# Linear attention plus gated feed-forward on one core: features kept token-major, turns moved from TensorE to DMA, key-value sums accumulated over all tiles, residual added by VectorE, start rebuilt

## Chip, cores and metric

One core of a Trainium2 chip. The time is the device time of one execution in microseconds (us), lower is better.

## The reference

One input x (2048 tokens of 512, bf16) is layer-normalised and goes into two branches whose results are added to x.

```python
xn = layernorm(x)
# branch A: 32 heads of 16
q, k, v = split_heads(xn @ wqkv)                       # wqkv 512 x 1536
pq, pk = q @ w_phi[h], k @ w_phi[h]                    # w_phi 16 x 16 per head
phi_q = concat(softmax(pq), softmax(-pq))              # 32 features per head
phi_k = concat(softmax(pk), softmax(-pk))
kv = phi_k.T @ v ;  z = sum over tokens of phi_k       # per head: 32 x 16 and 32
o = (phi_q @ kv) / (phi_q @ z + 1e-6)
A = o @ wo                                             # 512 x 512
# branch B
B = ((xn @ w_gate) * (xn @ w_up)) @ w_down             # 512 -> 1792 -> 512
out = x + A + B
```

## The kernel before

It is already tuned: a helper records each operation with its reads and writes, and a list scheduler orders the engines. Tokens are handled in 16 tiles of 128. `w_phi` is folded into `wqkv` on the chip, so one matmul group gives pq or pk. The parts that matter here:

Words used below: a *turn* is a transpose; a *unit* is the gate product, the up product and their elementwise product for one of the 14 feature tiles and 512 (or 256) tokens; the *numerator* of a tile is its `phi_q @ kv`; *K steps* are the key tiles' stretch of the program, and the *hand-over* is the point where it passes to the query tiles (the q stage). A *hole* is a time in which TensorE waits, and *filler* is work that may be put there. In the profiles PE is TensorE, PEld its weight loads, DVE VectorE, ACT ScalarE, POOL GpSimd and SP the queue that issues DMA.

```python
# (1) normalisation: statistics of four tiles, then a Newton iteration on GpSimd (cut)
for it in range(3):
    pool(... tv = src * src); pool(... tv = tv * veps)
    pool(... tv = tv * -0.5 + 1.5); pool(... yv = src * tv)

# (2) x, the projection weights, the q features and o are all turned on TensorE
def emit_xT(t):
    for q in range(NQ):
        items.append((bank(b, q * 128, 128), xn_tile(t)[:, q * 128:(q + 1) * 128], ident))
    mm_multi(items)
    act_op(out_ap, bank(b)...)                         # eviction on ScalarE

# (3) key-value sums: all 16 key tiles first, then 8 groups of 16 matmuls, 129 wide
for t in range(NT):
    pairs.append((ek_v[:, side, t, c * 128:(c + 1) * 128], vext_all[:, t, c, :]))
mm_group(out_ap, pairs)                                # out_ap: 128 x 129

# (4) per query tile: 8 turns, 8 numerators (128 wide), 8 denominators (8 wide), 4 turns of o
for side in range(2):
    src = ering(slot, 0) if side == 0 else enr(slot)
    ... items.append((bank(tb[side], c * 128, 128), src[:, c * 128:(c + 1) * 128], ident))
for c in range(NQ):
    mm_group(bank(bo, c * 128, 128), [(eT_all[:, r, side * 4 + c, :], kvbd_v[:, c * 2 + side, :]) for side in range(2)])
for c in range(NQ):
    mm_group(bank(tb[0], c * 8, 8), [(eT_all[:, r, side * 4 + c, :], zbd_v[:, c * 2 + side, :]) for side in range(2)])

# (5) output: 14 down products, 4 of wo, and the residual as identity x x, in one accumulator
n_terms = NF + NQ + 1
for i, t in enumerate(tiles):
    acc_mm(i, ident, x_tile(t))
```

Of the 14 feature tiles of the gated branch five are computed early in units of 512 tokens; the other nine come in units of 256 tokens just before their down products.

The softmax here doesn't subtract the row's maximum and nothing guards it: scores larger than these inputs give would overflow.

## Time and profile before

| | before |
|---|---|
| time, median of the first 3 runs | 270.84 us (269.82 to 273.06) |
| span of the profiled execution | 270.5 us |
| TensorE busy | 246.2 us, 91% |
| VectorE, ScalarE, GpSimd busy | 58%, 47%, 20% |

From the page of the kernel before: the busy table; TensorE (PE), its granted clock and DMA in 40 slices (each digit is tenths); and the shares of the chain of work that ended last.

```profile
span 270.5 us, 4879 instructions
PE 246.2 (91%) x1902; PEld 156.7 (58%) x1936; DVE 156.2 (58%) x364; ACT 128.1 (47%) x261; POOL 53.8 (20%) x99
PE   0068999999999999999999999999999999999994
PEclk9999999999999999999999999999999999999999
DMA  6999300000000000000000001001001010000101
...
PE 80%; DVE 8%; ACT 3%; DMA 3%; issue 3%; POOL 2%; DVEq 0%; POOLq 0%
```

PE is the limit from the fifth slice on, at full clock. The table of stretches of the same kernel shows what is lost before that (columns: stretch, its length, busy us and instructions of each engine, granted clock, DMA share, GB/s):

```profile
0.00:14.90 14.90, 0.01 (x1) 0.01 (x1) 10.14 (x36) 1.28 (x1) 8.00 (x38) 1.00 0.88 282
14.90:38.00 23.10, 19.71 (x148) 12.91 (x151) 11.11 (x33) 18.84 (x36) 7.84 (x31) 1.00 0.66 240
...
180.00:268.00 88.00, 86.21 (x571) 55.39 (x579) 24.37 (x54) 21.59 (x53) 0.00 (x0) 1.00 0.05 16
```

In the first 38 us the trace has 112 transposes (at 56 ns, 6.3 us of streaming) and 36 matmuls of 512 columns (at 216 ns, 7.8 us): about 14 us of work at full rate, an estimate from the counts and the spacing below. A 128-wide record lasts 240 ns on average where neighbours can start 56 ns apart, so small matmuls that alternate with evictions look busy. The clock column reads 1.00 where the trace has no clock record yet, and the first one is at 27.24 us. The starts of neighbouring transposes lie 107 ns apart until 26.7 us and 56 ns apart from 27.9 us on: half rate, then full. Eight transposes before and after (start, length):

```profile
14.89 1.04 PE L323 MATMUL ps<-arena 128*128 128x128 bf16 x8 [14.89 <-POOL arena L450]
101.77 0.61 PE L323 MATMUL ps<-arena 128*128 128x128 bf16 x8
```

The spacing of matmuls is read where the chain runs through PE without a break. From the chain of the kernel before, in order of time (start, length, what):

```profile
186.99 2.68 PE ps L654 x12
189.67 0.87 PE ps L309 x8
```

L654 are 512 columns wide (223 ns each here; the median distance of neighbouring starts in the trace is 216), L309 here 256 (109 ns each).

### The profile page before, as it was taken

How to read it: one execution, taken by the hardware profiler on the slowest of the kernel's cores; microseconds unless marked ns; L12 is line 12 of the kernel's file. 1: busy time of each engine (PE TensorE's matmuls, PEld its weight loads, DVE VectorE, ACT ScalarE, POOL GpSimd, SP SyncE). 2: the span in 40 equal slices, each digit the busy share in tenths (PEclk: the TensorE clock that was granted, in tenths of full speed). 3: DMA queues.
4: the chain of work that ended last, by engine and by line, in shares of the span. 5: the costliest groups of instructions: out<-in, count | busy, mean ns of one | idle time of the engine just before them, and what ended most of it. 6: DMA issues, size and time to landing. Idle time of an engine off the chain costs nothing.

```text
span 270.5 us, 4879 instructions
## 1 busy us (share of the span) xinstructions
PE 246.2 (91%) x1902; PEld 156.7 (58%) x1936; DVE 156.2 (58%) x364; ACT 128.1 (47%) x261; POOL 53.8 (20%) x99
## 2 busy tenths in 40 slices
PE   0068999999999999999999999999999999999994
PEld 0046544444444587777567765775766757566661
DVE  3951699989797985787677776542232323313231
ACT  1057898646665704776665755632222313222221
POOL 4560253333442430313112131100000000000000
PEclk9999999999999999999999999999999999999999
DMA  6999300000000000000000001001001010000101
GB/s 198 351 393 381 119 0 1 2 0 0 0 0 2 0 4 2 0 2 0 22 19 2 4 1 41 0 2 39 0 2 39 2 39 0 26 15 2 39 1 39
DMA packets 9446, 12.12 MB, mean 45 GB/s; under 512 B 448, under 2 KB 8400, under 8 KB 9424
## 3 DMA queue, kind: packets, MB, share of 16 engines
q1 hardware_dynamic: 9392, 11.80, 12.6%
q8 instruction: 15, 0.25, 0.4%
q0 software_dynamic: 32, 0.02, 0.1%
q14 instruction: 7, 0.06, 0.1%
HBM read 9.72 MB, written 2.10 MB: 44 GB/s over the span
## 4 chain that ended last, share of the span: by engine, by line
PE 80%; DVE 8%; ACT 3%; DMA 3%; issue 3%; POOL 2%; DVEq 0%; POOLq 0%
PE ps L309 50%; PE ps L654 24%; PE ps L323 7%; ACT arena L287 3%; DMA arena<-in_A_w_phi_dram 3%; DVE arena L499 2%; DVE arena L506 1%; DVE arena L534 1%; DVE arena L504 1%; POOL arena L395 1%; DVE arena L465 1%; DVE arena L576 0%; DVE arena L679 0%; DVE arena L457 0%; POOL arena L449 0%
## 5 line engine op out<-in xcount | busy, mean ns | idle before, releaser
L287 ACT ACTIVATE arena<-ps 128x512 bf16<-128x512 f32 (+1 forms) x260 | 126.9, 541 | 138.9 <-PE ps L309 92.9
L309 PE MATMUL ps<-arena 128*128 128x256 bf16 (+4 forms) x1300 | 172.6, 279 | 1.6 <-ACT arena L287 0.5
L309 PEld LDWEIGHTS ps<-arena 128*128 128x128 bf16 x1312 | 109.0, 98 | 59.0 <-PE ps L309 2.2
L654 PE MATMUL ps<-arena 128*128 128x512 bf16 x282 | 77.9, 381 | 2.0 <-DVE arena L679 0.6
L679 DVE TENSOR_TENSOR arena<-ps,arena 128x256 bf16<-128x256 f32 x72 | 30.0, 416 | 55.3 <-PE ps L654 52.9
L323 PE MATMUL ps<-arena 128*128 128x128 bf16 x320 | 30.9, 240 | 17.6 <-POOL arena L450 14.9
L654 PEld LDWEIGHTS ps<-arena 128*128 128x128 bf16 x304 | 28.0, 97 | 24.4 <-PE ps L654 4.4
L323 PEld LDWEIGHTS ps<-arena 128*128 128x128 bf16 x320 | 24.4, 107 | 27.1 <-DMA arena<-in_A_wqkv_dram 14.9
L506 POOL TENSOR_TENSOR arena<-arena 128x512 bf16<-128x512 bf16 x16 | 22.6, 1413 | 34.6 <-DVE arena L504 26.3
L584 POOL TENSOR_TENSOR arena<-arena 128x512 bf16<-128x512 bf16 x16 | 16.9, 1056 | 63.0 <-DVE arena L582 47.0
L576 DVE TENSOR_REDUCE arena<-arena 128x32 f32<-128x512 bf16 x32 | 20.6, 678 | 7.3 <-ACT arena L287 7.2
L499 DVE TENSOR_REDUCE arena<-arena 128x32 f32<-128x512 bf16 x32 | 20.6, 678 | 6.0 <-ACT arena L287 6.0
L534 DVE TENSOR_TENSOR arena<-ps,arena 128x512 bf16<-128x512 f32 x20 | 13.6, 682 | 1.5 <-PE ps L309 1.4
L432 DVE BATCH_NORM_STATS2 arena<-arena 128x6 f32<-128x512 bf16 x16 | 10.5, 684 | 4.8 <-DMA arena<-in_A_x_dram 4.8
L707 DVE CAST arena<-ps 128x512 bf16<-128x512 f32 x8 | 5.5, 692 | 12.4 <-PE ps L654 12.3
L506 DVE TENSOR_TENSOR arena<-arena 128x512 bf16<-128x512 bf16 x16 | 11.6, 728 | 0.4
L465 DVE TENSOR_SCALAR arena<-arena 128x512 bf16<-128x512 bf16 x16 | 5.8, 410 | 9.8 <-PE ps L323 9.8
L621 DVE TENSOR_TENSOR arena<-ps,arena 128x512 bf16<-128x512 f32 x16 | 10.9, 682 | 0.3
L504 DVE RECIPROCAL arena<-arena 128x64 f32<-128x64 f32 x16 | 8.8, 550 | 0.4
L618 DVE SCALAR_TENSOR_TENSOR arena<-arena,ps 128x32 f32<-128x32 f32 x16 | 3.0, 188 | 10.3 <-PE ps L309 10.1
L620 DVE RECIPROCAL arena<-arena 128x32 f32<-128x32 f32 x16 | 5.6, 351 | 0.4
L581 DVE RECIPROCAL arena<-arena 128x32 f32<-128x32 f32 x16 | 5.6, 348 | 0.4
(31 smaller groups left out, 30.3 us busy)
## 6 DMA issues: line engine op xcount, KB each, us to landing
arena<-in_A_x_dram SPq DMA_DIRECT2D x4, 512.0 KB, 6.6
out_dram<-arena SPq DMA_DIRECT2D x16, 128.0 KB, 1.7
arena<-in_B_w_gate_dram SPq DMA_DIRECT2D x1, 1792.0 KB, 12.0
arena<-in_B_w_up_dram SPq DMA_DIRECT2D x1, 1792.0 KB, 15.2
arena<-in_B_w_down_dram SPq DMA_DIRECT2D x1, 1792.0 KB, 18.1
arena<-in_A_wqkv_dram SPq DMA_DIRECT2D x3, 512.0 KB, 11.2
arena<-in_A_wo_dram SPq DMA_DIRECT2D x1, 512.0 KB, 8.9
arena<-in_A_w_phi_dram POOLq DMA_DIRECT2D x1, 16.0 KB, 7.5
```

What stands on the lines that cost most here:

```text
L287: return e.activation(out=out_ap, in_=in_ap, func=func, scale=scale, **kw)
L309: ins = e.matmul(out_ap, lhsT=l, rhs=r, start=(i == 0), stop=(i == n - 1))
L323: ins = e.matmul(o, lhsT=l, rhs=r, start=True, stop=True)
L499: dve(lambda e, side=side: e.tensor_reduce(out=sm[:, side * 32:(side + 1) * 32], in_=ering(slot, side).rearrange("p (h f) -> p h f", f=16) ...
L504: dve(lambda e: e.reciprocal(out=rs, in_=sm), [sm], [rs])
L506: fn = (lambda e, side=side: e.tensor_tensor(out=ek_v[:, side, t, :].rearrange("p (h f) -> p h f", f=16), in0=ering(slot, side).rearrange( ...
L534: dve(lambda e: e.tensor_tensor(out=dest_ap, in0=bank(bu), in1=gring(slot), op=ALU.mult), [bank(bu), gring(slot)], [dest_ap])
L576: dve(lambda e, side=side: e.tensor_reduce(out=sm[:, side * 32:(side + 1) * 32], in_=ering(slot, side).rearrange("p (h f) -> p h f", f=16) ...
L584: pool(lambda e: e.tensor_tensor(out=enr(slot).rearrange("p (h f) -> p h f", f=16), in0=ering(slot, 1).rearrange("p (h f) -> p h f", f=16) ...
L621: dve(lambda e: e.tensor_tensor(out=oring(slot).rearrange("p (h d) -> p h d", d=16), in0=bank(bo).rearrange("p (h d) -> p h d", d=16), in1 ...
L654: return e.matmul(o, lhsT=lhsT, rhs=rhs, start=first, stop=last)
L679: dve(lambda e: e.tensor_tensor(out=h, in0=bank(bu, 256, 256), in1=g, op=ALU.mult), [bank(bu, 256, 256), g], [h])
```

## The change

The intent: take everything off TensorE that is not a product of the reference. Features of both signs are made side by side in one 1024-wide token-major tile, reduced once, and turned by one DMA per tile; x (from tile 4 on), o and the projection weights are turned by DMA too. Key-value sums are accumulated over all key tiles in two PSUM banks, with the denominators as 4 extra columns (68 wide). Gated units of 512 tokens are spread among key and value steps and down products. The residual is added by VectorE as it evicts the accumulator. The start is rebuilt: small loads of x in front, `rstd` from two ScalarE operations, dummy matmuls, and 256-token gated units while the weights arrive. The order on TensorE is now fixed by the program; a planner orders the other engines.

```diff
@@ turns, and the start @@
-        items.append((bank(b, q * 128, 128), xn_tile(t)[:, q * 128:(q + 1) * 128], ident))   # all tiles
+            if turn:
+                sc.dma(SP, o, xn_tile(t), 131072, turn=True, reads=[xn_tile(t)], writes=[o], name=f"xT{t}")
+        act_op(lnv_v[:, a:b], mv_v[:, a:b, 1], func=ACTF.Ln, bias=eps_f, name=f"ln{a}")
+        act_op(rstd_v[:, a:b], lnv_v[:, a:b], func=ACTF.Exp, scale=-0.5, name=f"rs{a}")
+    WARM(14)
+    ...                                    # T(0), T(1), WARM(2), U2(0, 0), U2(1, 0), ..., FOLD(1)
@@ features @@
+        act_op(ev[:, :, 0, :], src, func=ACTF.Exp, name=f"{name}e{t}")
+        act_op(ev[:, :, 1, :], src, func=ACTF.Exp, scale=-1.0, name=f"{name}e{t}")
+        dve(... tensor_reduce(out=sm, in_=Et as 64 groups of 16 ...), cost=1130.0)
+        pool(... ev[:, :, 1, :] *= ratio ...)
+        sc.dma(SP, qT_v[:, t % NQT, :, :], Et, 262144, turn=True, ...)            # query tiles
@@ key-value sums @@
+        mm([(kvb(c), Et[:, c * 128:(c + 1) * 128], vext_v[:, t % 4, c, :], t == 0 and c % 4 == 0, t == NT - 1)
+            for c in range(8)], name=f"kv{t}")
@@ V's eviction takes the key normalisation @@
+        dve(... o1 = src * rp_ ...)                    # 512 wide, from PSUM
+        dve(lambda e: e.tensor_copy(out=ve[:, :, 64:68], in_=rp_), ...)           # 32 values
@@ q stage, one tile per turn of the loop @@
+        NUM(t + 1)                                     # 8 matmuls, 68 wide, then VectorE, then a DMA turn of o
+        some(0.4)                                      # gated units
+        DOWN(t, 0, 7)
+        Q(t + 3)
+        DOWN(t, 7, NF)
+        some(1.0)
+        WO(t)
+        FIN(t)                                         # VectorE: out = accumulator + x
... (scheduler, buffer layout and the last tile's split into halves are cut)
```

## The prediction

> **What bounds it now.** TensorE. The busy table: PE 246.2 of 270.5 us (91%), DVE 58%, ACT 47%, POOL 20%; the chain of waits is 80% PE; granted clock 1.00. By stretches: before 14.9 us PE waits (normalisation needs a 512 KB x load, then a Newton chain on POOL); from 14.9 to 38 us it is busy 19.7 of 23.1, small transposes alternating with evictions; from 38 to 268 us it is over 98% busy; the tail after the last matmul is 3 us.
>
> **Cost of a matmul**, from the timeline's starts: eight 128x256 take 0.87 us (109 ns each), four 128x512 0.87 us (217 ns), eight 128x128 plus eight 128x8 0.65 us (about 56 and 25 ns). This agrees with the Trainium skill, "TensorE: Matmul & The Clock Gate", section "Back-to-back issue gap" (N/2.4 + 2.5 ns).[...]
>
> **What goes.** In streamed PE columns: weight transposes 4,096; x transposes of 12 of 16 tiles 6,144; q-feature transposes 16,384; o transposes 8,192; residual 8,192; key-value 16,512 -> 8,704; numerator and denominator 17,408 -> 8,704. About 558,000 columns become 498,500: at 217 ns per 512, 25 us[...]. Estimated PE work: 241 -> 213 us (878 of N=512, 190.5; 100 of 256, 10.9; 48 of 128, 2.7; 256 of 68 at an estimated 31 ns, 8).
>
> **What moves.** Turns to DMA: 12 x 128 KB, 1 MB of weights, 16 x (256+128) KB, 8.5 MB. The Trainium skill, "DMA: Bandwidth & Descriptors", section "Latency and other measured facts", gives 261 GB/s for a non-contiguous DMA transpose: an estimated 33 us of DMA, which was nearly idle from 38 us on. No run shows that yet; the turns have 8 to 14 us before their readers. DVE: two 678 ns reduces become one of about 1.2 us; gated products become 512 wide (682 ns for 2 x 416); V's eviction (682) takes the ek scaling; the residual joins the eviction (0.69). DVE stays at 155 to 160 us, but in the first eight K steps needs about 4.9 us per step against PE's 5.1. ACT falls to about 105.
>
> **Start.** x comes in 128 KB pieces and rstd is two short ACT operations: the first gated matmuls can start at 7 to 8 us, on a warmed clock, filling PE while weights land.
>
> **Sum.** First real work 7.5 + PE work 213 + start-up holes 3 + DVE-bound waits in the K steps 4 + hand-over to the q stage 1.5 + tail 2.5 = about 232 us. Nearly all removed PE work is on the critical path, since PE is it.
>
> **Predicted: 232 us, 8 in 10 between 225 and 243.** Faster by over 2%: 0.97; within 2%: 0.02; slower: 0.01.
>
> **Right if** PE stays over 90% busy and leads the chain; no PE transposes after about 10 us; 68-wide matmuls spaced near 31 ns; DMA under 3 tenths in the steady part; waits for turns near zero; first gated matmul before 9 us. **Wrong steps would show** as PE waiting on a turn (SP's in-order queue, or turns far slower than the change's assumed 190 GB/s), PE waiting on DVE in the K steps[...].
>
> **What would make it wrong.** Upward: slow turns, turns issued one by one, weights pushed back by them, DVE shortage. Downward: less stalling than allowed, about 225.

## More of the kernel before

A piece of the chain goes by line, and one line can mix shapes: the piece of 103 matmuls in 7.29 us at 94.65 us holds 96 of 129 columns and seven of 512. The starts of the 129-wide ones lie 55 to 60 ns apart.

## The result and the profile after

| | before | after |
|---|---|---|
| time, median | 271.38 us (269.82 to 273.06, 4 runs) | 235.37 us (234.42 to 236.37, 4 runs) |
| ratio | | 0.8667 (0.8616 to 0.8719) |
| span of the profiled execution | 270.5 | 232.5 |
| PE busy | 246.2 | 219.9 |
| ACT busy | 128.1 | 77.0 |
| DVE busy | 156.2 | 159.3 |

All outputs are right. The ratios are from fast runs in the same rounds; they are not quite the ratio of the quoted medians. Where kernels that ran on different chips are compared below, their ratios to the kernel before are subtracted and multiplied by 271 us. Each ratio is known to about 0.003 (95%), so such a difference is known to about 1.2 us.

The page after, same parts:

```profile
span 232.5 us, 3320 instructions
PE 219.9 (95%) x1298; PEld 108.7 (47%) x1298; DVE 159.3 (69%) x306; ACT 77.0 (33%) x153; POOL 38.8 (17%) x52
PE   7797999999999999995999999999999999999785
PEclk9999999999999999998899999999999999999999
DMA  6999997401000000006230443243074217304321
...
PE 77%; DMA 9%; DVE 8%; ACT 2%; SPq 1%; issue 1%; POOL 0%
```

PE still leads the chain. Two dents are new: one in the nineteenth slice (with a lowered clock after it) and one near the end. The waits of PE name them (who waits for whom: us in total, times, longest):

```profile
PE ps L448 <- DMA arena<-arena: 5.3, 3, 2.5
PE ps L448 <- ACT arena L420: 1.7, 1, 1.7
PE ps L448 <- DVE arena L525: 1.5, 1, 1.5
PE ps L448 <- DVE arena L597: 0.8, 1, 0.8
PE ps L448 <- DVE arena L573: 0.4, 1, 0.4
PE ps L448 <- DVE arena L694: 0.3, 1, 0.3
```

"DMA arena<-arena" is a turn. The timeline of PE from 102 us on shows where (in brackets the idle time before):

```profile
106.23 0.43 PE L448 MATMUL ps<-arena 128*128 128x68 bf16 x8 [0.86 <-DMA arena<-arena]
108.54 110.62 PE L448 MATMUL ps<-arena 128*128 128x68 bf16 x600 [1.88 <-DMA arena<-arena]
221.67 8.24 PE L448 MATMUL ps<-arena 128*128 128x68 bf16 x62 [2.52 <-DMA arena<-arena]
```

The first two are the first numerators of the q stage, the third is the last numerator. The stretches after:

```profile
0.00:38.00 38.00, 33.56 (x205) 18.55 (x206) 29.79 (x71) 18.07 (x45) 8.04 (x23) 1.00 1.04 270
38.00:102.00 64.00, 63.68 (x411) 31.28 (x409) 56.84 (x102) 28.94 (x56) 13.86 (x15) 1.00 0.10 18
102.00:112.00 10.00, 7.26 (x40) 3.21 (x39) 6.87 (x14) 2.73 (x5) 3.18 (x3) 0.83 0.48 92
112.00:218.00 106.00, 106.00 (x582) 49.86 (x580) 62.37 (x114) 27.25 (x48) 13.77 (x13) 1.00 0.32 63
```

From 112 to 218 us PE ran 478 matmuls of 512 columns and 104 of 68 without a gap. Neighbouring starts lie 216 and 30 ns apart (medians of the trace), which makes 106 us, so PE is at its streaming rate there and the 68-wide ones do not wait for weight loads. In the first 38 us PE now does about 27 us of work: 64 matmuls of 256 columns (7.0 us), 32 of 128 (1.8 us) and an unbroken 18.5 us from 19.45 us on; before it did 14.

So the gain of 38 us in the span has these parts, by count and spacing (estimates from the traces): about 29 us less PE work (240 us before, 211 after without the dummies), about 13 us more of it done in the first 38 us, and about 7 us given back in new holes (2.7 and 2.5 us of waits for turns, and about 1.7 us of half clock after the first). The rest, about 3 us, is in small gaps: from 38 us to its last matmul the kernel before did about 226 us of work in 229.4.

### The profile page after: what moved, and what is told of

The parts are those of the page before. It is cut to its first block, busy times and chain, and to the rows that moved or that the text cites. A ratio compares the mean times of both kernels' runs of the same rounds, so it can differ in the third digit from the quotient of the medians.

```text
span 232.5 us, 3320 instructions
## 1 busy us (share of the span) xinstructions
PE 219.9 (95%) x1298; PEld 108.7 (47%) x1298; DVE 159.3 (69%) x306; ACT 77.0 (33%) x153; POOL 38.8 (17%) x52
## 4 chain that ended last, share of the span: by engine, by line
PE 77%; DMA 9%; DVE 8%; ACT 2%; SPq 1%; issue 1%; POOL 0%
PE ps L448 77%; DMA arena<-arena 7%; DMA arena<-in_A_x_dram 2%; ACT arena L420 2%; DVE arena L573 1%; DVE arena L565 1%; DVE arena L694 1%; DVE arena L626 1%; SPq L168 1%; DVE arena L655 1%; SPq L167 1%; POOL arena L634 0%; DVE arena L644 0%; DVE arena L785 0%; DVE arena L743 0%
## 5 line engine op out<-in xcount | busy, mean ns | idle before, releaser
L448 PE MATMUL ps<-arena 128*128 128x512 bf16 (+3 forms) x1298 | 219.9, 332 | 10.0 <-DMA arena<-arena 5.3
L448 PEld LDWEIGHTS ps<-arena 128*128 128x128 bf16 x1298 | 108.7, 99 | 121.0 <-DMA arena<-arena 6.4
L420 ACT ACTIVATE arena<-ps 128x512 bf16<-128x512 f32 (+1 forms) x134 | 72.3, 585 | 129.6 <-PE ps L448 129.0
L626 DVE TENSOR_REDUCE arena<-arena 128x64 f32<-128x1024 bf16 x32 | 38.8, 1214 | 40.0 <-ACT arena L420 39.9
L634 POOL TENSOR_TENSOR arena<-arena 128x512 bf16<-128x512 bf16 x32 | 33.9, 1059 | 175.9 <-DVE arena L632 175.9
L694 DVE TENSOR_TENSOR arena<-ps,arena 128x512 bf16<-128x512 f32 x52 | 35.5, 682 | 8.0 <-PE ps L448 7.3
L768 DVE TENSOR_TENSOR arena<-ps,arena 128x512 bf16<-128x512 f32 x15 | 10.4, 691 | 6.7 <-PE ps L448 6.6
L743 DVE TENSOR_TENSOR arena<-ps,arena 128x512 bf16<-128x512 f32 x16 | 11.1, 691 | 0.6
L655 DVE TENSOR_TENSOR arena<-ps,arena 128x512 bf16<-128x512 f32 x16 | 10.9, 682 | 0.0
L658 DVE CAST arena<-arena 128x32 bf16<-128x32 f32 x16 | 10.0, 623 | 0.0
L632 DVE TENSOR_TENSOR arena<-arena 128x32 f32<-128x32 f32 x32 | 6.0, 188 | 0.8
L420 ACT ACTIVATE arena<-arena 128x2 f32<-128x2 f32 (+1 forms) x18 | 4.2, 250 | 6.4 <-DVE arena L567 6.2
L705 DVE TENSOR_TENSOR arena<-ps,arena 128x256 bf16<-128x256 f32 x8 | 3.4, 419 | 2.6 <-ACT arena L420 2.6
L785 DVE TENSOR_TENSOR arena<-ps,arena 128x256 bf16<-128x256 f32 x2 | 0.8, 424 | 2.8 <-PE ps L448 2.8
```

Source lines behind the costliest of these rows:

```text
L420: return e.activation(out=out_ap, in_=in_ap, func=func, scale=scale, **kw)
L448: ins = e.matmul(o, lhsT=l, rhs=r, start=s, stop=p, skip_group_check=True)
L626: dve(lambda e: e.tensor_reduce(out=sm, in_=Et.rearrange("p (h f) -> p h f", f=16), axis=AX.X, op=ALU.add), [Et], [sm], cost=1130.0, name= ...
L634: pool(lambda e: e.tensor_tensor(out=ev[:, :, 1, :], in0=ev[:, :, 1, :], in1=ratio[:, :, None].to_broadcast([128, H, 16]), op=ALU.mult), [ ...
L655: dve(lambda e: e.tensor_tensor(out=o1, in0=src, in1=rp_[:, :, :, None].to_broadcast([128, 8, 4, 16]), op=ALU.mult), [src, rs_v[:, t % 4, ...
L658: dve(lambda e: e.tensor_copy(out=ve[:, :, 64:68], in_=rp_), [rs_v[:, t % 4, :]], [ve[:, c, 64:68] for c in range(8)], cost=90.0, name=f"v ...
```

## Experiments

Two theories were set against each other. Theory: PE is the limit nearly everywhere, so a column put on it costs its streaming time, and the start and the new holes count one for one. Rival: the gain is one of order and start, and PE's work in the steady part has slack.

The runs came in three groups of four, each on one chip.

### e1: the changed kernel again

No edit.

> The changed kernel again, unedited, as the yardstick of this chip for the runs beside it. Both theories: 234 to 237 us. In its first four runs it took 234.4 to 234.6 us at a mean granted clock of 0.993 and 236.1 to 236.4 us at 0.985, so two modes are expected again, about 1.7 us apart, each with its own clock.

Measured: 234.61 us median (233.98 to 236.31). Both modes came: 233.98 to 234.80 us at a mean clock of 0.993 in four runs, 235.99 and 236.31 us at 0.985 in two. The profiled execution was one of the latter. Its stretches after the two holes (the granted clock is the third number from the end; 1.00 is full):

```profile
108.00:112.00 4.00, 3.53 (x18) 1.53 (x19) 1.79 (x5) 0.60 (x1) 0.19 (x1) 0.68 0.50 98
112.00:116.00 4.00, 4.00 (x18) 1.72 (x17) 0.56 (x2) 1.08 (x2) 0.00 (x0) 0.89 0.15 33
220.00:224.00 4.00, 2.24 (x13) 0.96 (x14) 1.23 (x3) 0.00 (x0) 0.00 (x0) 0.76 0.41 90
224.00:228.00 4.00, 4.00 (x18) 1.83 (x17) 0.20 (x1) 0.00 (x0) 0.00 (x0) 0.81 0.15 35
```

Each hole is followed by a stretch of lowered clock: (1 - 0.68) x 4 + (1 - 0.89) x 4 = 1.7 us lost after the first and as much after the second. That is half clock for 3.4 us, and it accounts for the step between the two modes. The Trainium skill, "TensorE: Matmul & The Clock Gate", section "Part 1: The HAM clock gate", describes this: half rate, decided over a free-running window of 3413 ns. The length agrees: both stretches of half clock in this trace last 3.41 us. The advice in its section "Why this matters for your kernels", to avoid gaps over about 3 us, is too generous here: holes of 2.5 us, or of 0.9 and 1.9 us with eight small matmuls between them, were enough in some executions and not in others (the profiled execution of e4 has two waits of 0.85 and 1.87 us at the hand-over and a clock of 1.00).

### e2: the residual back on TensorE

```diff
-        return [(..., wo_v[:, q, :], False, q == NQ - 1) for q in range(NQ)]
+        return [(..., wo_v[:, q, :], False, False) for q in range(NQ)] + [(bank(b), ident, x_tile(t), False, True)]
-        dve(lambda e: e.tensor_tensor(out=o, in0=bank(b), in1=x_tile(t), op=ALU.add), ...
+        dve(lambda e: e.tensor_copy(out=o, in_=bank(b)), [bank(b)], [o],
```

> Undoes one part: the residual goes back to TensorE as a 17th... 19th term (identity times x) of 15 of the 16 output tiles' accumulators and two halves of the last; VectorE only copies. Theory (removed TensorE columns are worth their streaming time, because TensorE is never idle in that stretch): 16 x 216 ns = 3.4 us slower than the unedited kernel beside it. Rival (the gain came from the early start and the new order, TensorE work in the steady part is hidden or has slack): within 0.5 us.

Measured: 235.12 us median, only 0.5 us above e1. The edit reached 15 tiles, not 16 (1,313 matmuls for 1,298), so the dose is 15 x 216 ns = 3.2 us; the expectation was wrong in that. At first sight the rival wins. But the executions must be compared at equal clock: with one drop (0.993) e2 took 235.69 to 236.48 us, mean 236.1, against a mean of 234.3 in e1, so 1.7 us more; and three of its six executions had no drop at all. PE's waits in its trace give the rest:

```profile
PE ps L448 <- DMA arena<-arena: 3.7, 3, 1.9
```

The waits for turns fell from 5.2 to 3.7 us: the extra matmuls stood in front of the last turn and filled its hole. The result cannot decide until the hole is gone; e6 repeats it.

### e3: more filler before the q stage

```diff
     Q(2)
     nextU()
+    nextU()
+    nextU()
     ring_banks[0] = [0, 1, 2, 3]
```

> Two more gated units (1.73 us each) are placed between the last feature tile and the first numerator, taken from the q stage; nothing is added or removed. Theory (the hand-over hole of 2.7 us is the wait for the first feature turn, and the half clock after it, some 1.7 us, is its consequence): hole gone, mean clock 0.997 or more, 3.5 to 4.5 us faster than the unedited kernel. Rival (turns go one after the other through one queue, so the hole only moves to the next numerator): under 1.5 us faster, with a wait on a turn a few us later.

Measured: 233.02 us, 1.6 us faster than e1, with the clock at 1.00 in two executions of six and 0.993 in four. Both theories were half right. The waits for turns at the hand-over vanished, but a hole of 1.7 us came back at the second numerator, and it is not a turn. The chain of e3 there (pieces of "issue", 0.02 to 0.05 us, left out):

```profile
108.70 0.69 DVE arena L694
109.39 0.10 DVE arena L737
109.52 0.36 DVE arena L739
109.91 0.70 DVE arena L743
110.66 1.51 PE ps L448 x13
```

The two numerators stand next to each other and use the same banks; the second must wait until VectorE has evicted the first. One unit belongs between them.

### e4: order at the end

```diff
-        if t + 1 < NT:
+        if t + 1 < NT and t != 14:
             NUM(t + 1)
...
-        DOWN(t, 0, 7)
         if t + 3 < NT:
             Q(t + 3)
+        DOWN(t, 0, 7)
+        if t == 14:
+            NUM(t + 1)
         DOWN(t, 7, NF)
```

> Only the order on TensorE: q features for tile t+3 are computed before the down products of tile t instead of in their middle (1.5 us earlier), and the last numerator comes after 7 of the 14 down products of tile 14 instead of before all. Theory (the 2.5 us hole near the end is the last feature turn, which has only about 7 us of work in front of it): hole under 0.5 us, 2 to 2.5 us faster. Rival (the chain of the last tile is as long as the remaining work, the hole reappears before the last output products): under 1 us faster.

Measured: 230.69 us, 3.9 us faster than e1 by the medians. PE waits only 2.7 us for turns, in two waits at the hand-over; the end hole is gone. The gain exceeds the hole of 2.5 us because a possible clock drop after it is gone too: three executions had no drop, three had one, none had two. At equal clock (0.993) e4 took 231.11 to 232.44 us, mean 231.8, against 234.3: 2.5 us, the hole itself.

### e5: both orders

On top of e4, one unit more before the first numerator and one between the first and the second:

```diff
     Q(2)
     nextU()
+    nextU()
     ring_banks[0] = [0, 1, 2, 3]
...
     NUM(0)
+    nextU()
     for t in range(NT):
```

> The end order of e4 plus a hand-over order: one gated unit more before the first numerator and one between the first and the second (in e3 two stood before the first, and the hole of 1.7 us came back as the second numerator's wait for VectorE to empty the banks of the first). Nothing added or removed on any engine. Theory (the remaining 2.7 us of waits for turns, and the drops to half clock that such holes set off in some runs, are ordering only): no wait of PE over 0.5 us after 20 us, clock 1.00 in every run, 227 to 228 us. Rival (the first turns of the q stage are limited by the queue): a hole of over 1 us somewhere before 115 us and 229 us or more.

Measured: 228.35 us (227.96 to 228.70), ratio 0.8435; clock 0.999 or 1.00 in all executions, and one mode instead of two. PE's waits:

```profile
PE ps L448 <- ACT arena L420: 1.7, 1, 1.7
PE ps L448 <- DVE arena L525: 1.5, 1, 1.5
PE ps L448 <- DVE arena L597: 1.4, 1, 1.4
PE ps L448 <- DVE arena L694: 1.1, 2, 0.5
PE ps L448 <- DVE arena L573: 0.4, 1, 0.4
```

No wait for a turn is left, and nothing longer than 0.53 us after 20 us. No work was removed: the order of some 75 matmuls (52 of the q features, 16 of two units, 8 of the last numerator) was worth (0.8642 - 0.8435) x 271 = 5.6 us against e1. This is the base for what follows.

### e6: the residual on TensorE, without a hole to hide in

The edit of e2 on top of e5.

> The residual on TensorE again (as e2), but on top of e5, where no hole near the end can swallow it. Theory (TensorE columns are worth their streaming time): 16 x 216 ns = 3.4 us slower than e5, give or take 0.5. In e2 the same edit showed only about 1.8 us at equal clock because the end hole shrank from 2.5 to 0.9 us. Rival (the residual's columns are worth less than their streaming time): again under 2 us.

Measured: 231.48 us, 3.1 us above e5 on the same chip, for a dose of 15 x 216 ns = 3.2 us. The theory holds, and e2's small effect was the hole.

### e7: the small cast twice

```diff
         dve(lambda e: e.tensor_copy(out=ve[:, :, 64:68], in_=rp_), ...
+        dve(lambda e: e.tensor_copy(out=ve[:, :, 64:68], in_=rp_), ...
```

> On top of e5: the small cast of 32 reciprocals per key tile (0.62 us on VectorE) is done twice, 16 x 0.62 = 10 us more VectorE work in the K steps, same result. Theory (VectorE is 10.0 of 10 us busy from 20 to 60 us, so the K steps are balanced on a knife's edge: the predicted DVE-bound waits of 4 us only just did not come): 3 to 7 us slower than e5, PE waiting on VectorE lines. Rival (the normalisations are done eight tiles ahead and can slip, VectorE has reserve): under 1 us slower.

Measured: 228.60 us, 0.25 us above e5. This does not answer the question: VectorE's busy time rose by only 1.3 us (159.5 to 160.8), not 10. The second cast adds about 0.08 us each. So the first one's 0.62 us is not its own work, which e9 looks into. The dose failed; e10 gives a real one.

### e8: no dummy matmuls at the start

```diff
-    WARM(14)
-    WARM(2)
```

> On top of e5: the 16 dummy matmuls at the start are removed. Theory (they bring the granted clock up before the first gated units): first useful work at the same time, but matmuls at half rate for some 3 us from there, 1.5 to 3 us slower than e5. Rival (the start is paced by loads, normalisation and evictions, so the clock there does not matter): under 0.7 us.

Measured: 229.13 us (228.02 to 229.29), 0.8 us above e5 by the medians and 0.5 by the ratios (0.8452 and 0.8435); the ranges overlap, so the times alone do not settle it. The first gated unit starts at 8.28 us instead of 8.62, but the pair of key features that PE reaches after the same wait for ScalarE comes at 21.27 us instead of 19.48. The trace shows why: the 256-wide matmuls start 213 ns apart until 14.0 us and 109 ns apart after that, where e5 has 109 ns from its first unit on. So half the theory holds: the dummies do bring PE to full rate before the first unit (in the changed kernel their own spacing falls from 427 to 216 ns at about 6 us), and without them the units lose about 3 us at half rate. Little of that reaches the end: in the two profiled executions the same matmul comes 1.8 us later after the early units, and 0.95 us later from 47 us on, because PE's wait for VectorE at 41.5 us in e5 does not come in e8. In time the dummies are worth about a microsecond at most.

### e9: two more orders

Fold after five early units instead of eight, and the cast before the GpSimd product:

```diff
-    for ft in range(4):
-        U2(ft, 256)
-    LN([4, 5])
-    LN([6, 7])
-    FOLD(1)
+    U2(0, 256)
+    FOLD(1)
+    for ft in range(1, 4):
+        U2(ft, 256)
+    LN([4, 5])
+    LN([6, 7])
...
+        z = dve(lambda e: e.tensor_copy(out=vz, in_=vp), ...)     # moved from V(t) to K(t)
         even_up(ev, sm, rv[:, :, 1], ratio, "k", t, z)             # the product waits for it
```

> On top of e5, two orders that are read apart in the trace. (a) The weights' fold comes after five instead of eight early gated units, so that its four evictions run beside the other three units: theory, the 1.7 us in which TensorE waits for ScalarE before the first key tile goes, 1 to 1.7 us faster; rival, the turned weights are not there yet and the wait moves ahead of the fold. (b) The cast of 32 reciprocals per key tile is issued before the GpSimd product instead of beside it. In the traces so far it takes 623 ns and ends with that product, and the second cast of e7 added only 0.08 us each. Theory (the cast waits for the GpSimd product to release what both need): 60 to 150 ns each, VectorE some 8 us less busy in the K steps, and no time gained by that, because TensorE does not wait there. Rival (the cast is slow by its shape): still about 620 ns. Time 226.5 to 227.5 us.

Measured: 227.50 us, ratio 0.8396, which is (0.8435 - 0.8396) x 271 = 1.1 us better than e5, about as much as the noise of such a difference. It is the lowest median. (a) The wait for ScalarE at the fold is gone, but a wait of 1.7 us for VectorE stands at 40.8 us (0.53 us in e5), so less than the hole was gained. (b) From the changed kernel's timeline, a GpSimd product and the cast beside it, then the cast's group there and in e9:

```profile
97.99 1.06 POOL L634 TENSOR_TENSOR arena<-arena 128x512 bf16<-128x512 bf16 x1 [4.38 <-DVE arena L632]
98.42 0.65 DVE L658 CAST arena<-arena 128x32 bf16<-128x32 f32 x1
```

```profile
L658 DVE CAST arena<-arena 128x32 bf16<-128x32 f32 x16 | 10.0, 623 | 0.0
```

```profile
L649 DVE CAST arena<-arena 128x32 bf16<-128x32 f32 x16 | 2.8, 175 | 0.3
```

The cast ended within 0.02 us of the product (99.07 and 99.05), and it takes 175 ns once it is issued ahead of it. The changed kernel itself holds the control: 15 of its 16 casts run beside a product, take 646 to 656 ns and end within 0.04 us of it; the one at 38.49 us has no product beside it and takes 167 ns. The Trainium skill, "SBUF — State Buffer", section "Who interferes with whom", says that a cast can take both VectorE port pairs, that one is shared with GpSimd as an exclusive lock, and that issue order decides who waits. This agrees: 623 against 175 ns for 32 elements. VectorE's busy time fell by 7 us, but the time only by 1.1 us with (a) included, so those 7 us were mostly not on the critical path. How the gain divides between (a) and (b) was not separated.

### e10: the key reciprocal twice

```diff
         dve(lambda e: e.reciprocal(out=rs, in_=sm), [sm], [rs], cost=500.0, name=f"kc{t}")
+        dve(lambda e: e.reciprocal(out=rs, in_=sm), [sm], [rs], cost=500.0, name=f"kc{t}")
```

> On top of e5: each key tile's reciprocal (0.54 us on VectorE) is done twice. e7 was meant as such a dose and added only 1.3 us in all. Now 16 x 0.48 = about 8 us are really added, half of it while the eight-tiles-ahead normalisations run. Theory (the K steps are balanced on a knife's edge): 2 to 5 us slower than e5, PE waiting on VectorE lines before 65 us. Rival (the normalisations can slip, there is reserve): under 1 us.

Measured: 230.95 us, ratio 0.8527, so (0.8527 - 0.8435) x 271 = 2.5 us (give or take 1.2) above e5 for 7.3 us more VectorE work (159.5 to 166.8). PE now waits for V's eviction:

```profile
PE ps L448 <- DVE arena L656: 3.2, 3, 1.9
```

Two of these three waits, 1.0 and 1.9 us, are at 38 and 43 us, where the normalisations still run; the last, 0.3 us, is at 77 us. So there was almost no reserve in the first half of the key steps and most of it in the second.

### e11: the start undone

x as four loads of 512 KB in front, gate and up weights as one load each, and no early 256-token units (their work comes later in 512-token units):

```diff
-    load_x(SP, 0, 1)
-    load_x(SP, 1, 1)
-    load_gu(SP, "g", 0, 2)
-    ... (pieces of x, gate and up weights in turn)
+    for g in range(4):
+        load_x(SP, 4 * g, 4)
+    load_wT(1); load_sq(SP, wv_v, ...)
+    load_gu(SP, "g", 0, NF)
+    load_gu(SP, "u", 0, NF)
...
-    U2(0, 0); U2(1, 0)
     LN([2, 3], turn=False); T(2); T(3)
-    U2(2, 0); U2(3, 0)
-    for ft in range(4):
-        U2(ft, 256)
```

> On top of e5, the start alone as in the kernel before: x in four loads of 512 KB ahead of all weights, gate and up weights as one load each, and no early gated units of 256 tokens (their work is done as 512-token units later). TensorE's work is the same. Theory (filling the load time with gated units is a part of the gain of its own): the first gated unit waits until about 20 us, 6 to 10 us slower than e5. Rival (the start is hidden, only the removed TensorE columns count): under 2 us slower.

Measured: 238.10 us, ratio 0.8786, so (0.8786 - 0.8435) x 271 = 9.5 us above e5, with the same work. PE now waits for loads, and the last one ends at 22.9 us:

```profile
PE ps L448 <- DMA arena<-in_B_w_up_dram: 2.6, 1, 2.6
PE ps L448 <- DMA arena<-in_B_w_gate_dram: 2.3, 1, 2.3
```

The mean clock was 0.971 (0.964 in one execution), because PE was at half clock from 13.71 to 27.36 us. Two stretches of this trace:

```profile
14.00:23.00 9.00, 3.62 (x8) 0.94 (x10) 6.84 (x21) 3.60 (x13) 1.06 (x1) 0.50 1.05 382
23.00:27.00 4.00, 4.00 (x10) 1.43 (x11) 1.12 (x2) 0.00 (x0) 0.00 (x0) 0.50 0.99 273
```

From 22.94 us on PE has no more waits, but its first ten matmuls of 512 columns still start 427 ns apart: 2.2 of the 9.5 us are half clock on work, an estimate from the spacing. The edit changes the loads, the early units and, through the waits, the clock together.

### e12: o turned on TensorE

```diff
-        sc.dma(SP, dst, o, 131072, turn=True, reads=[o], writes=[dst], name=f"oT{t}")
+    def OT(t):                             # before WO(t - 1), one tile ahead of its reader
+        mm([(bank(b, q * 128, 128), o[:, q * 128:(q + 1) * 128], ident, True, True) for q in range(NQ)], ...)
+        act_op(oT_v[:, t % 4, :, :], bank(b).rearrange("p (q s) -> p q s", q=NQ), name=f"oe{t}")
```

> On top of e5: the 16 turns of o (128 KB each) go from the DMA queue back to TensorE, as 64 transposes of 128x128 and 16 evictions on ScalarE, which has time. Theory (a turn on TensorE costs its streaming time, a turn on DMA nothing): 64 x 56 ns = 3.6 us slower than e5. Rival (TensorE transposes hide, or DMA turns delay something themselves): within 1 us, or faster.

Measured: 231.48 us, ratio 0.8547, so 3.0 us (give or take 1.2) above e5 for an expected 3.6. ScalarE's busy time rose by 9.6 us (77.0 to 86.6) and cost nothing that shows. In the order of e5 a turn of o by DMA costs no time that shows, and a turn on PE costs about its streaming time.

## Why the prediction was right

It said 232 us, 225 to 243; measured were 235.37. Point by point:

- **PE is the limit, and removed columns count in full: right, and shown for two parts.** The residual is worth 3.1 us (e6), the turn of o 3.0 us (e12). The other parts of the 29 us (q turns, weight turns, the narrower key-value and numerator products) rest on the same price per column and were not undone one by one.
- **"PE work 213": right.** In the profiled execution the first gated unit starts at 8.58 us and the last matmul ends near 229.5. Minus the holes in between (7.7 us) and the half clock (1.7 us) this leaves about 212 us. One input of the sum was misread: it had put a 129-wide product at 71 ns, from the chain piece that mixes shapes, and booked 3 us with fewer instructions for that. The trace has 58 ns on average. The slip did no harm: by count at the spacing of the trace the work falls from 240 to 211 us, where the prediction had 241 to 213.
- **"First real work 7.5": 8.58 us.** (The last transposes of x on TensorE start at 11.4 us, where "about 10" was said.) "Start-up holes 3": 2.1 us (0.4 and 1.7). That the start is a gain of its own is shown by e11 (9.5 us); the rest of the 13 us more work done in the first 38 us was not tested: the Newton chain, the alternation of transposes and evictions, and the half rate at which the kernel before ran its transposes until 27 us. The "warmed clock" was real, since the first unit runs at full rate, but e8 shows that it was worth about a microsecond at most in the order of e5.
- **"DVE-bound waits in the K steps 4": this term was mis-sized, 0.3 us.** The reason behind it was sound: VectorE was busy 10.00 of 10 us in stretches between 20 and 60 us, and e10 shows that 7.3 us more work there costs 2.5 us. The balance just held, and it held although the cast in V's eviction took 0.62 us a tile where the planner of the changed kernel counts 0.09 us.
- **"Hand-over to the q stage 1.5": 2.7 us,** plus about 1.7 us of half clock. The prediction foresaw a wait here, but neither that two numerators in a row share banks (e3) nor the clock drop.
- **"The turns have 8 to 14 us before their readers ... waits for turns near zero": wrong.** The waits were 5.3 us, in the two holes of the hand-over and one near the end. At the end only about 7 us stand between the features of tile 15 and their reader, because the gated units are used up by then; the hole of 2.5 us was missing from the sum. e4 shows that it was order alone.
- **Span and time.** The sum was one of the span and came out within 1 us of it (232.5). The timed execution is longer than its span by 2.1 us after (234.6 for 232.5), and by 1.7 us before (271.42 for 269.7 in one run). Together with the second clock drop of half the runs this is the 3 us between 232 and 235.4. That the sum came so close is luck in part: the K steps, the start-up holes and the PE work took some 6 us less than their terms, and the first unit, the hand-over with its half clock, the end hole and the tail (3.0 us) took some 7 us more.
- **"ACT falls to about 105": wrong, 77.0.** ScalarE was nowhere near the limit, so the time does not show it.
- **68-wide matmuls near 31 ns: right,** 30 ns. **DMA under 3 tenths in the steady part: just missed,** 0.32. The turns were dearer than estimated. In the trace the packets of 256 bytes are the turns: 34,816 of them, 8.91 MB, took 51.3 us of the 16 DMA engines' time. That is 174 GB/s, not the 261 GB/s that I took from the Trainium skill.

## What to carry to other kernels

When TensorE is at its streaming rate, count columns (and check the price of each shape on neighbouring starts, since a line of a chain can mix shapes): each transpose, identity product or double sum that moves elsewhere returns its streaming time, provided that the engine that takes it has room at that very moment. After such a rebuild look for the places where filler runs out (stage changes, last tile), for there a new latency shows, and a hole of 2.5 us on TensorE can cost 4 us because the clock drops after it. And when undoing a part shows no effect, look whether a hole has swallowed it before believing that the part was worth nothing.

## What the Trainium skill lacked or had wrong

- "TensorE: Matmul & The Clock Gate", section "Why this matters for your kernels", advice to avoid idle gaps over about 3 us: a hole of 2.5 us, or 0.9 and 1.9 us with eight small matmuls between, set off the half clock in some executions (1.7 us lost each time, which is half of the page's window of 3413 ns). For kernel authors it lacks that a kernel may show two times for this reason: 234.3 and 236.2 us in e1, one time of 228.4 us in e5 without these holes.
- The same page, section "Back-to-back issue gap", gives about 131 ns for a sustained 512-column matmul and about 81 ns for 128 columns. Here 512 columns cost 216 ns back to back, and transposes of 128 columns start 56 ns apart (the 64 of e12 added 3.0 us). Its other formula, N/2.4 + 2.5, fits these two, and the 109 ns of 256 columns, the 30 of 68 and the 55 to 60 of 129.
- "DMA: Bandwidth & Descriptors", section "Latency and other measured facts": 261 GB/s for a non-contiguous turn. Here 174 GB/s by the time of the packets (turns of 128 and 256 KB in SBUF, and two of 512 KB from DRAM).
- "SBUF — State Buffer", section "Who interferes with whom", had the shared port right (623 against 175 ns); nothing to correct.
- None of the pages gives the difference between the span of the program's instructions and the timed execution: 1.7 us before, 2.1 us after.
- No page says that the granted clock of a trace reads full before its first clock record: in the kernel before it reads 1.00 until 27 us, while transposes start 107 ns apart.
